# Attention with beacon keys and an ELU MLP on one core: sums of exp tiles and masks for both head pairs in one instruction, and a new written-out order

## The chip, the cores and the metric

The kernel runs on one core of a Trainium2 chip. Its engines work side by side: PE (TensorE, matmuls; PEld is its load of weights, which overlaps), DVE (VectorE), ACT (ScalarE), POOL (GpSimd) and SP (SyncE, which here only issues DMAs). The metric is the device time of one execution in microseconds, as the median of several runs.

## What is computed

Eight batches of attention with eight heads, 576 queries, 16 beacon keys ahead of 576 causal keys, and head size 64; then one MLP with an ELU on all 4608 tokens.

```python
# q, k, v: (8, 8, 576, 64); beacon_k, beacon_v: (8, 8, 16, 64)
k_all = concatenate([beacon_k, k], axis=2); v_all = concatenate([beacon_v, v], axis=2)
scores = where(causal, -1e9, q @ k_all^T / 8)      # beacons are never masked
a = exp(scores - max); a /= a.sum(-1) + 1e-9
x = (a @ v_all) as 4608 tokens x 512
h = x @ w_in                                       # 512 -> 2048
out = where(h > 0, h, exp(min(h, 0)) - 1) @ w_out  # 2048 -> 512, float32
```

## The kernel before

**Tiles.** The 592 keys of a batch stand in five chunks of up to 128 rows (the last has 80). Scores are computed with keys on the partitions, so that exp gives tiles that P·V takes as they are; only the causal part of each chunk is kept, 928 + 672 + 416 + 160 and, for the first chunk, 1152 columns for the two heads of a pair. The eight heads are four pairs, two pairs a group, and a group's exp tiles lie in one SBUF tile `et`. The MLP's 4608 tokens are tiles of 512 (the first cut in two halves, so the order counts tiles 0 to 9).

**Steps.** The order of the work is written out by hand: a list of words in `run(...)` (lines 790 on), each a small function with its arguments, and every engine runs its instructions in exactly that order. A word such as `S.3.6` is the function S for batch 3, piece 6. The words that matter here:

- `lq`, `T`, `cq`, `ck`: for batches 0 to 2, load q and k and transpose them on PE. From batch 3 on, `lk` (line 754) copies q (`.0`) or k (`.1`) of a batch into a scratch in HBM as bf16, issued by POOL, and `lt` (line 761) brings it back with DMA transposes issued by SP, two in a step, one step per group of heads, into the one pair of tiles `stq[1]`; `lp` (lines 769 and 770) fills the rest of the k tile: a memset and a copy of the beacon keys on POOL.
- `lv` (lines 144 and 149): the loads of V, five chunks and the beacons, issued by POOL into a tile `v16` that has two buffers. `wi` and `wo` (lines 161 and 165): the loads of the two weights, 16 and 4 pieces.
- `S` (line 320): scores on PE. `x` (335): exp on ACT. `m` (340): the causal mask, a multiplication on DVE.
- `D` (line 393), from batch 3 on: DVE adds a head pair's exp tiles over the chunks, so that `L` (lines 377 and 419) takes the row sums with one matmul a head from the result; `L` also does the first 112 queries of P·V. `n` (434, 437): reciprocals on ACT. `W` (377): the other queries of P·V. `M` (471): scaling on DVE into the MLP's input `xT`.
- `F` (511): the first MLP matmul, 4 x 128x512. `e`, `u` (521, 526) on ACT and `k`, `r`, `g` (536, 543, 548) on DVE: the ELU.
- `G` (557), tiles 0 and 1: the second MLP matmul. `Q` (621), the other tiles: the same in a form with seven instead of eight block products; `wt` and `Z` (578) are its additions on DVE, `J` (630, 635, 637) the drains of its sums, with stores issued by SP from a buffer `osb`. `H`, `X`, `P`, `K`, `E`, `U`, `V` do the first MLP matmul of the last two tiles in the same form.
- `o`, `s` (564, 570): drain and store of tiles 0 and 1.

POOL's transfers use eight completion semaphores in turn: each transfer is issued only when the one issued eight before it has landed.

The sums of `D` go to `presum[b, p]`, which is the buffer of a head pair that the transposes of batches 0 to 2 had used:

```python
r_ = presum[b, p] = qks[p % 2].bitcast(FP16)[:, :, 0:S]
...
o = r_[0:rows, :, a:e]
(nc.vector if eng == "v" else nc.gpsimd).tensor_tensor(
    out=o, in0=t[0:rows, :, a:e] if n == 0 else o, in1=t[0:rows, :, col:col + e - a], op=ALU.add)
```

Of the kernel before, what the change touches and what calls it, by code (L numbers as in the profile page):

```python
# [9 lines left out]
FP16 = mybir.dt.float16  # L10
# [7 lines left out]
def kernel(  # L18
# [134 lines left out]

# [3 lines left out]
    def load_wi(c):  # L157
        f_ = slice(DF // 2 * c, DF // 2 * (c + 1))
        for g in range(2):
            for i in range(4):  # L160
                nc.gpsimd.dma_start(
                    out=w_in16[32 * i:32 * (i + 1), 2 * g:2 * g + 2, f_], in_=wi_v[i, :, g, :, f_])
# [18 lines left out]
    qks = [konst.tile([P, 2, P * NKC], BF16, name=f"qk{i}") for i in range(2)]  # L181
# [67 lines left out]
    @step  # L249
    def wi(c):  # L250
        load_wi(c)
# [87 lines left out]
    def mask(o, i):  # L339
        nc.vector.tensor_tensor(out=o, in0=o, in1=i, op=ALU.mult)  # L340
# [5 lines left out]
    def m(b, p, g):  # L346

        t = et(b, p)
        if b > 0:
            m_ = lambda c: triu[:, c:c + 2, :].unsqueeze(1).broadcast_to([P, 2, 2, P])  # L350
            if g == 0:
                mask(t[:, :, 0:2 * C1].rearrange("p h (j c) -> p h j c", j=2)[:, :, :, 0:P], m_(0))
            else:
                n_ = C3 - C2
                mask(t[:, :, C2 - n_ + P:C3 + P].rearrange("p h (j c) -> p h j c", j=2)[:, :, :, n_ - P:n_], m_(1))
                mask(t[0:kc[4], :, C4:ECOLS], triu[0:kc[4], 1:3, 0:ECOLS - C4])
            return
# [27 lines left out]
    @step  # L385
    def D_(b, p, n, eng="v"):

        r_ = presum[b, p] = qks[p % 2].bitcast(FP16)[:, :, 0:S]
        t = et(b, p)
        a, e, col = next((a, e, col) for (j, a, e, col) in lays[b] if j == n + 1)  # L390
        rows = kc[n + 1]
        o = r_[0:rows, :, a:e]
        (nc.vector if eng == "v" else nc.gpsimd).tensor_tensor(  # L393
            out=o, in0=t[0:rows, :, a:e] if n == 0 else o, in1=t[0:rows, :, col:col + e - a], op=ALU.add)
# [6 lines left out]
    def L(b, g):  # L401
# [12 lines left out]
        else:  # L414
            t = hd[b, g] = psum.tile([P, 1024], FP32, tag="S", name="lt")
            r_ = lt[b, g] = t[:, 512 - QA:512 - QA + S]
            if b >= BD:
                for i in range(4):
                    nc.tensor.matmul(
                        out=r_[32 * i:32 * (i + 1), QA:S], lhsT=ones,  # L420
                        rhs=presum[b, 2 * g + i // 2][:, i % 2, QA:S], start=True, stop=True, skip_group_check=True)
# [374 lines left out]
    cb.1.3 r.0.4 g.0.4 e.1.7 r.1.7 lq.2.0.0.8 G.0.0.0 x.1.7 F.0.5 x.1.11 e.0.5 S.1.12 g.1.7
    cb.2.1 m.1.2.0 x.1.12 S.1.0 F.0.7 r.0.5 G.0.1.0 S.1.8 x.1.0 g.0.5 F.1.5 e.0.7 x.1.8 m.1.3.1
    S.1.10 cb.2.0 m.1.1.1 S.1.9 e.1.5 x.1.10 r.0.7 g.0.7 cb.2.2 lv.1.0.1 wo.1 r.1.5 g.1.5 x.1.9
    F.1.0 u.1.0 e.1.0 m.1.0.0 T.2.0.0 cq.2.0.0 F.0.3 T.2.1.0 cq.2.1.0 T.2.2.0 e.0.3 u.0.3
    m.1.2.1 k.0.3 wt.1.0 k.1.1 ck.2.2.0 F.1.4 F.0.6 e.0.6 S.2.0 S.2.5 x.2.5 x.2.0 r.0.6 m.1.3.0  # L800
    G.0.0.1 m.1.0.1 g.0.6 G.0.1.1 k.1.0 lv.1.2.3.4 lp.3.0 lp.3.1 T.2.3.0 e.1.4 ck.2.3.0 L.1.1
    n.1.1 F.1.2 r.1.4 u.1.2 e.1.2 M.1.1.0 W.1.1 M.1.1.1 S.2.3 F.1.3 x.2.3 L.1.0 W.1.0 n.1.0 wo.2
    M.1.0.0 M.1.0.1 u.1.3 e.1.3 wo.3 g.1.4 G.0.0.2 S.2.1 x.2.1 F.2.13 wt.1.1 e.2.13 S.2.4 lk.3.0
    lk.3.1 lt.3.0 x.2.4 S.2.8 x.2.8 k.1.2 cb.2.3 G.0.1.2 F.2.0 u.2.0 u.2.13 S.2.7 x.2.7 k.1.3
    S.2.9 x.2.9 e.2.0 G.0.0.3 o.0.0 G.0.1.3 F.2.3 e.2.3 S.2.10 m.2.0.0 S.2.2 r.2.3 g.2.3 k.2.0
    x.2.10 x.2.2 G.1.0.0 F.2.11 e.2.11 u.2.11 S.2.6 S.2.12 lv.2.2.3.4 x.2.6 F.2.1 u.2.1 e.2.1
    m.2.1.0 F.1.6 G.1.0.1 m.2.2.1 x.2.12 k.2.13 F.2.7 e.2.7 m.2.0.1 m.2.1.1 k.2.11 u.2.7 k.2.7
    u.1.6 lv.2.0.1 e.1.6 G.1.0.2 S.3.0 x.3.0 S.2.11 x.2.11 F.2.9 F.2.15 e.2.9 H.1.1 o.0.1 u.2.15
    k.2.1 k.1.6 m.2.3.0 e.2.15 L.2.0 W.2.0 n.2.0 F.2.12 m.2.3.1 r.2.9 g.2.9 M.2.0.1 lk.5.1 F.2.6
    M.2.0.0 G.1.0.3 lk.4.0 wt.2.0 wt.2.1 m.2.2.0 e.2.6 u.2.6 wt.4.1 s.0.0 s.0.1 u.2.12 e.2.12  # L810
    k.2.15 S.3.2 S.3.3 x.3.3 F.2.4 F.2.14 x.3.2 k.2.12 u.2.14 L.2.1 n.2.1 W.2.1 e.2.4 M.2.1.0
    M.2.1.1 e.2.14 u.2.4 G.1.1.0 S.3.4 F.2.2 lv.3.0.1 F.2.8 k.2.4 k.2.14 x.3.4 k.2.6 e.2.2 u.2.2
    e.2.8 r.2.8 m.3.0.1 S.3.1 o.1.0 k.2.2 lt.3.1 S.3.5 x.3.5 F.2.10 e.2.10 G.1.1.1 x.3.1 u.2.10
    G.1.1.2 m.3.0.0 lk.4.1 D.3.0.0 S.3.8 x.3.8 S.3.6 x.3.6 k.2.10 g.2.8 D.3.0.1 lt.4.0 Z.2.3.0
    F.3.12 m.3.1.0 D.3.1.0 m.3.1.1 e.3.12 G.1.1.3 H.1.2 D.3.1.1 u.3.12 S.3.9 o.1.1 s.1.1 S.3.11
    x.3.11 F.2.5 u.2.5 F.3.3 Q.2.0.7 e.2.5 k.2.5 x.3.9 k.3.12 Z.2.1.0 S.3.10 e.3.3 x.3.10 u.3.3
    k.3.3 F.3.1 Q.2.7.14 Z.2.2.0 m.3.2.1 Q.2.14.21 e.3.1 S.3.12 S.3.7 lt.4.1 u.3.1 x.3.12 F.3.13
    F.3.9 J.2.0.v x.3.7 e.3.13 Q.2.21.28 D.3.1.2 D.3.1.3 Z.2.3.1 Q.2.28.35 e.3.9 u.3.9 k.3.9
    D.3.0.2 D.3.0.3 k.3.1 wt.3.1 u.3.13 k.3.13 m.3.3.0 lp.4.0 S.4.4 x.4.4 S.4.0 F.3.0 x.4.0
# [113 lines left out]
```

## Time and profile before

| | |
|---|---|
| median of 3 runs | 337.73 us (336.92 to 338.57) |
| span of the profiled execution | 335.3 us, so about 2.4 us of the median lie around the span |
| PE | 324.6 us busy, 97%, 3561 matmuls |
| ACT | 282.5 us busy, 84% |
| DVE | 280.0 us busy, 84%, 592 instructions |
| POOL | 87.9 us busy, 26% |
| q0 (POOL's transfers) | 18.49 MB, mostly packets under 512 B |
| q1 (SP's) | 15.34 MB |

The profile is one execution, taken by the hardware profiler. Its page gives the busy time of each engine, the same in 40 equal slices (a digit is tenths of a slice, 9 for 90% or more; a slice here is 8.4 us), and groups of instructions by line and shape: `out<-in`, shape, count, then busy us and mean ns of one, then the idle time ahead of them and who ended it. A list of waits names for each engine and line whom it waited for, with the sum, the number and the longest. A list by windows gives, for a stretch of the span, the busy us of each engine, the mean clock of PE, the DMA share and the GB/s.

### The profile page before, as it was taken

The page shows a single profiled execution, that of the slowest core. Times are in us where ns is not written, and L with a number is a line of the kernel's source. Part 1 is how long each engine was busy: PE and PEld are TensorE (multiplying, and loading weights), DVE is VectorE, ACT ScalarE, POOL GpSimd, SP SyncE. Part 2 cuts the span into 40 slices and gives each one's busy share as a digit, 9 for nine tenths or more (in the row PEclk, how much of TensorE's full clock was granted, in tenths as well). Part 3 has the DMA queues.
Part 4 walks back from the last instruction along what each step waited for, and adds up shares of the span by engine and source line. Part 5 has one row for each costly group of instructions (what it writes and reads, how often), then busy time and mean ns, then how long its engine had stood idle before and what let it go on. Part 6 is the DMA issues. An engine that isn't in the chain of part 4 may idle for free.

```text
span 335.3 us, 8722 instructions
## 1 busy us (share of the span) xinstructions
PE 324.6 (97%) x3561; PEld 206.8 (62%) x3561; DVE 280.0 (84%) x592; ACT 282.5 (84%) x460; POOL 87.9 (26%) x121
## 2 busy tenths in 40 slices
PE   7979899999999999999999999999999999999995
PEld 3546666454446555657555656556555888688784
DVE  3652988666899999997999889988999998998962
ACT  2998798899999999989898889897987677988930
POOL 8875749360049106500160060000000000000000
PEclk9997999999999999999999999999999999999999
DMA  9999999999939997996099495000101021010212
GB/s 114 146 174 178 165 186 186 157 147 176 149 52 170 175 139 61 171 149 105 33 140 139 104 100 139 3 33 31 39 27 34 31 65 65 31 65 31 65 63 96
DMA packets 129080, 34.65 MB, mean 103 GB/s; under 512 B 112912, under 2 KB 127504, under 8 KB 129040
## 3 DMA queue, kind: packets, MB, share of 16 engines
q0 software_dynamic: 94912, 18.49, 68.6%
q1 hardware_dynamic: 33408, 15.34, 21.2%
q8 instruction: 28, 0.46, 0.6%
q10 hardware_dynamic: 720, 0.26, 0.3%
q14 instruction: 12, 0.10, 0.1%
HBM read 37.22 MB, written 15.34 MB: 157 GB/s over the span
## 4 chain that ended last, share of the span: by engine, by line
PE 53%; DVE 20%; ACT 11%; DMA 7%; POOL 4%; issue 3%; ACTq 0%; POOLq 0%
PE ops L621 20%; PE hps L511 16%; DVE gt L536 6%; PE hps L691 6%; DVE qk L393 5%; ACT et L335 4%; ACT e L521 3%; PE sc L320 3%; PE ops L557 3%; ACT r L526 3%; PE ut L377 3%; DMA v<-in_v_dram 2%; DMA kst<-in_k_dram 2%; DMA w_out<-in_moe_w_out_dram 2%; DVE et L340 2%
## 5 line engine op out<-in xcount | busy, mean ns | idle before, releaser
L511 PE MATMUL hps<-xT,w_in 128*128 128x512 f16 (+1 forms) x544 | 120.2, 357 | 0.7 <-DMA w_in<-in_moe_w_in_dram 0.5
L335 ACT ACTIVATE et<-sc 128x1024 f16<-128x1024 f32 (+2 forms) x114 | 104.7, 978 | 5.3 <-PE sc L320 5.3
L621 PEld LDWEIGHTS <-gt 128*128 128x128 f16 x768 | 74.1, 98 | 18.7 <-issue 1.7
L521 ACT ACTIVATE e<-hps 128x512 f32<-128x512 f32 x120 | 72.5, 622 | 7.7 <-PE hps L511 5.9
L511 PEld LDWEIGHTS <-w_in 128*128 128x128 f16 x544 | 49.8, 98 | 45.3 <-issue 7.9
L536 DVE SCALAR_TENSOR_TENSOR gt<-e,r 128x512 f16<-128x512 f32 x108 | 71.9, 682 | 6.7 <-ACT r L526 4.4
L526 ACT ACTIVATE r<-hps 128x512 f16<-128x512 f32 x108 | 65.3, 623 | 7.7 <-PE hps L511 4.4
L621 PE MATMUL ops<-wt,gt 128*128 128x256 f16 x384 | 50.1, 273 | 0.0
L621 PE MATMUL ops<-w_out,gt 128*128 128x256 f16 x384 | 49.6, 273 | 0.4 <-DVE osb L635 0.3
L149 POOL DMA_DIRECT2D v<-in_v_dram x40 | 36.0, 1048 | 5.5 <-DMA w_out<-in_moe_w_out_dram 2.4
L340 DVE TENSOR_TENSOR et<-et,triu 128x512 f16<-128x512 f16 (+4 forms) x108 | 31.6, 331 | 1.5 <-ACT et L335 1.5
L578 DVE TENSOR_TENSOR gt<-gt 128x1024 f16<-128x1024 f16 x48 | 32.4, 684 | 0.3
L393 DVE TENSOR_TENSOR qk<-qk,et 128x672 f16<-128x672 f16 (+2 forms) x60 | 21.8, 368 | 0.9
L377 PEld LDWEIGHTS <-v 128*32 128x32 f16 (+1 forms) x800 | 17.0, 96 | 8.7 <-issue 0.8
L377 PE MATMUL ut<-et,v 128*32 128x464 f16 (+3 forms) x560 | 21.0, 296 | 0.0
L637 DVE TENSOR_TENSOR osb<-ops,sm 128x512 f32<-128x512 f32 x24 | 16.4, 682 | 4.3 <-issue 3.3
L471 DVE TENSOR_TENSOR xT<-ut,rl 128x672 f16<-128x672 f32 (+12 forms) x26 | 16.4, 668 | 1.7 <-ACT rl L437 1.1
L621 PE MATMUL ops<-w_out,s 128*128 128x256 f16 x128 | 17.1, 273 | 0.0
L730 DVE SCALAR_TENSOR_TENSOR gt<-e,r 128x512 f16<-128x512 f32 x24 | 16.0, 685 | 0.8 <-ACT r L720 0.7
L144 POOL DMA_DIRECT2D v<-in_beacon_v_dram x8 | 6.5, 812 | 38.4 <-PE ut L377 38.4
L557 PE MATMUL ops<-w_out,gt 128*128 128x512 f16 x64 | 16.0, 380 | 0.6 <-DMA w_out<-in_moe_w_out_dram 0.6
L621 PEld LDWEIGHTS <-s 128*128 128x128 f16 x128 | 12.4, 98 | 3.0
(108 smaller groups left out, 394.8 us busy)
## 6 DMA issues: line engine op xcount, KB each, us to landing
out_dram<-osb SPq DMA_DIRECT2D x35, 256.0 KB, 2.3
v<-in_v_dram POOLq DMA_DIRECT2D x24, 128.0 KB, 7.1
scr<-in_q_dram POOLq DMA_DIRECT2D x5, 576.0 KB, 13.8
scr<-in_k_dram POOLq DMA_DIRECT2D x5, 576.0 KB, 15.4
w_in<-in_moe_w_in_dram POOLq DMA_DIRECT2D x16, 128.0 KB, 7.5
w_out<-in_moe_w_out_dram POOLq DMA_DIRECT2D x4, 512.0 KB, 9.4
v<-in_v_dram POOLq DMA_DIRECT2D x8, 112.0 KB, 9.7
v<-in_v_dram POOLq DMA_DIRECT2D x8, 80.0 KB, 6.7
```

Of the source, the lines that this page charges most:

```text
L149: nc.gpsimd.dma_start(out=vt[b][r0:r0 + n, j, :, :], in_=v[b, :, ilo[j]:ilo[j] + n, :].rearrange("h s d -> s h d"),)
L335: nc.scalar.activation(out=ets[b, d][:, :, a - EC2 * d:e - EC2 * d], in_=sc[b, g][:, :, a - c0:e - c0], func=AFT.Exp, bias=0.0, scale=SCALE)
L340: nc.vector.tensor_tensor(out=o, in0=o, in1=i, op=ALU.mult)
L377: nc.tensor.matmul(out=t[32 * i:32 * (i + 1), a - qa:e - qa], lhsT=ones[0:kc[j], :] if half is None else v16[0:kc[j], j, h, 32 * half:32 * ...
L393: (nc.vector if eng == "v" else nc.gpsimd).tensor_tensor(out=o, in0=t[0:rows, :, a:e] if n == 0 else o, in1=t[0:rows, :, col:col + e - a], ...
L511: nc.tensor.matmul(out=h[:, n_, :], lhsT=w_in16[:, cc, P * fc:P * (fc + 1)], rhs=xt[k][:, cc, a - TT * k:e - TT * k], start=(cc == 0), sto ...
L521: nc.scalar.activation(out=eb[t, i], in_=flat(hp[t, i]), func=AFT.Exp, bias=0.0, scale=1.0)
L526: nc.scalar.activation(out=rb[t, i], in_=flat(hp[t, i]), func=AFT.Relu, bias=0.0, scale=1.0)
L536: nc.vector.scalar_tensor_tensor(out=half(t, i), in0=eb[t, i], scalar=1.0, in1=rb[t, i], op0=ALU.subtract, op1=ALU.min)
L557: nc.tensor.matmul(out=ob[t, tb_], lhsT=gt[:, fc, P * tb_:P * (tb_ + 1)], rhs=w_out16[:, fc, :], start=(fc == 0), stop=(fc == NFC - 1))
L578: (nc.vector if eng == "v" else nc.gpsimd).tensor_tensor(out=o_, in0=a_, in1=b_, op=op_)
L621: nc.tensor.matmul(out=xy[t, n_][:, qd, :], lhsT=lw[:, P * qd:P * (qd + 1)], rhs=wt_[:, c, :], start=(first and qd == 0 and c == 0), stop= ...
```

## The change

1. `D` adds both head pairs of a group in one instruction: `D.b.p.n` becomes `D.b.g.n`, 80 instructions of 928, 672, 416 and 160 elements a partition become 40 of 1856, 1344, 832 and 320. The two buffers for the sums become one tile, and `L` reads its part of it. (A branch for batches under 3 is written but not used.)
2. `m`, for batches from 1 on, masks both pairs of a group at once: per batch 12 instructions become 6, those of 512 elements become 1024, those of 160 become 320.
3. The loads of V can be ordered chunk by chunk, with the beacons' load right behind chunk 0 rather than first; the loads of w_in are named one by one, in the same order as before.
4. The list of steps is new behind the first 160 or so. Matmuls, ACT's work and transfers are the same in number and bytes.

```diff
     def load_v(b, js):
         if b not in vt:
             vt[b] = stage.tile([P, NKC, H, D], FP16, tag="v16", name="v16")
-            nc.gpsimd.dma_start(
-                out=vt[b][0:NB, 0, :, :], in_=beacon_v[b].rearrange("h n d -> n h d"))
         for j in js:
...
+            if j == 0:
+                nc.gpsimd.dma_start(
+                    out=vt[b][0:NB, 0, :, :], in_=beacon_v[b].rearrange("h n d -> n h d"))
...
-    qks = [konst.tile([P, 2, P * NKC], BF16, name=f"qk{i}") for i in range(2)]
+    qk01 = konst.tile([P, 2, 2, P * NKC], BF16, name="qk01")
+    qks = [qk01[:, i, :, :] for i in range(2)]
...
-        t = et(b, p)
+        t = et(b, p) if b == 0 else None
         if b > 0:
-            m_ = lambda c: triu[:, c:c + 2, :].unsqueeze(1).broadcast_to([P, 2, 2, P])
+            t = ets[b, p].rearrange("p h (y c) -> p h y c", y=2)
+            m_ = lambda c: triu[:, c:c + 2, :].unsqueeze(1).unsqueeze(1).broadcast_to([P, 2, 2, 2, P])
             if g == 0:
-                mask(t[:, :, 0:2 * C1].rearrange("p h (j c) -> p h j c", j=2)[:, :, :, 0:P], m_(0))
+                mask(t[:, :, :, 0:2 * C1].rearrange("p h y (j c) -> p h y j c", j=2)[:, :, :, :, 0:P], m_(0))
...
-    def D_(b, p, n, eng="v"):
-
-        r_ = presum[b, p] = qks[p % 2].bitcast(FP16)[:, :, 0:S]
-        t = et(b, p)
+    def D_(b, g, n):
+
...
+            r_ = qk01.bitcast(FP16)[:, :, :, 0:S]
+        presum[b, g] = r_
+        t = ets[b, g].rearrange("p i (y c) -> p y i c", y=2)
...
-                        rhs=presum[b, 2 * g + i // 2][:, i % 2, QA:S], start=True, stop=True, skip_group_check=True)
+                        rhs=presum[b, g][:, i // 2, i % 2, QA:S], start=True, stop=True, skip_group_check=True)
```

The steps on POOL's queue between 33 us and the transfers of batch 5, in the order of issue:

```
before  wo.0 lq.2 lv.1.0.1 wo.1 lv.1.2.3.4 lp.3.0 lp.3.1 wo.2 wo.3 lk.3.0 lk.3.1 lv.2.2.3.4 lv.2.0.1
        lk.5.1 lk.4.0 lv.3.0.1 lk.4.1 lp.4.0 lv.3.2.3.4 lv.5 lp.4.1 lk.5.0 lk.6.0 lv.4 lk.6.1
after   wo.0 lq.2 wo.1 lv.1.1 lv.1.0 lv.1.4 lv.1.2 lp.3.0 lv.1.3 lk.3.1 lv.3.3 wo.2 lv.3.4 lk.3.0 wo.3
        lv.2.3 lv.2.2 lv.2.0 lp.3.1 lv.3.1 lv.2.4 lk.4.0 lv.2.1 lk.7.1 lk.7.0 lk.4.1 lk.6.1 lv.3.2
        lv.4.2 lv.3.0 lv.4.0 lv.4.3 lk.5.1 lp.4.0 lv.4.4 lk.5.0 lp.4.1 lk.6.0 lv.5.2 lv.4.1 lv.5.0
```

and on SP's:

```
before  lt.3.0 s.0.0 s.0.1 lt.3.1 lt.4.0 s.1.1 lt.4.1 J.2.1 lt.5.0 ... s.1.0 (beside tile 7)
after   lt.3.0 lt.3.1 s.0.0 lt.4.0 lt.4.1 s.0.1 J.2.1 s.1.0 lt.5.0 ...
```

The order of PE's steps around them, before:

```
G.0.0.2 S.2.1 F.2.13 S.2.4 S.2.8 G.0.1.2 F.2.0 S.2.7 S.2.9 G.0.0.3 G.0.1.3 F.2.3 S.2.10 S.2.2 G.1.0.0
F.2.11 S.2.6 S.2.12 F.2.1 F.1.6 G.1.0.1 F.2.7 G.1.0.2 S.3.0 S.2.11 F.2.9 F.2.15 L.2.0 W.2.0
```

and after:

```
G.0.1.1 G.0.1.2 S.2.6 S.2.1 F.2.0 F.2.11 S.2.4 S.2.10 G.0.0.1 G.0.0.2 F.1.6 F.2.13 S.2.2 S.2.9 F.2.3
G.0.1.3 L.2.0 F.2.15 F.2.9 S.2.11 S.2.12 G.0.0.3 F.2.1 S.2.8 S.2.7 G.1.0.0 F.2.7 G.1.0.1 F.2.6 S.3.3
S.3.0 F.2.14 F.2.12 W.2.0
```

More of the change, by code (lines that the diff above doesn't have):

```diff
@@ L152, in load_v, with load_wi @@
             )
+            if j == 0:
+                nc.gpsimd.dma_start(
+                    out=vt[b][0:NB, 0, :, :], in_=beacon_v[b].rearrange("h n d -> n h d"))
     wi_v = moe_w_in.rearrange("(g i t d) f -> i d g t f", i=4, t=2, d=32)
     wo_v = moe_w_out.rearrange("(f p) m -> p f m", p=P)
-    def load_wi(c):
+    def load_wi(c, n):
         f_ = slice(DF // 2 * c, DF // 2 * (c + 1))
[L159 to L162, printed above, removed]
+        g, i = n // 4, n % 4
+        nc.gpsimd.dma_start(
+            out=w_in16[32 * i:32 * (i + 1), 2 * g:2 * g + 2, f_], in_=wi_v[i, :, g, :, f_])
     def load_wo(i):
@@ L249, in wi @@
     @step
-    def wi(c):
-        load_wi(c)
+    def wi(c, n):
+        load_wi(c, n)
     @step
@@ L346, in m @@
     def m(b, p, g):
-        t = et(b, p)
+        t = et(b, p) if b == 0 else None
         if b > 0:
-            m_ = lambda c: triu[:, c:c + 2, :].unsqueeze(1).broadcast_to([P, 2, 2, P])
+            t = ets[b, p].rearrange("p h (y c) -> p h y c", y=2)
+            m_ = lambda c: triu[:, c:c + 2, :].unsqueeze(1).unsqueeze(1).broadcast_to([P, 2, 2, 2, P])
             if g == 0:
-                mask(t[:, :, 0:2 * C1].rearrange("p h (j c) -> p h j c", j=2)[:, :, :, 0:P], m_(0))
+                mask(t[:, :, :, 0:2 * C1].rearrange("p h y (j c) -> p h y j c", j=2)[:, :, :, :, 0:P], m_(0))
             else:
                 n_ = C3 - C2
-                mask(t[:, :, C2 - n_ + P:C3 + P].rearrange("p h (j c) -> p h j c", j=2)[:, :, :, n_ - P:n_], m_(1))
-                mask(t[0:kc[4], :, C4:ECOLS], triu[0:kc[4], 1:3, 0:ECOLS - C4])
+                mask(t[:, :, :, C2 - n_ + P:C3 + P].rearrange(
+                    "p h y (j c) -> p h y j c", j=2)[:, :, :, :, n_ - P:n_], m_(1))
+                mask(t[0:kc[4], :, :, C4:ECOLS],
+                     triu[0:kc[4], 1:2, 0:ECOLS - C4].unsqueeze(1).broadcast_to([kc[4], 2, 2, ECOLS - C4]))
             return
@@ L385, in D_ @@
     @step
-    def D_(b, p, n, eng="v"):
-        r_ = presum[b, p] = qks[p % 2].bitcast(FP16)[:, :, 0:S]
-        t = et(b, p)
+    def D_(b, g, n):
+        if b < BD:
+            r_ = stq[b % 2][g].bitcast(FP16)[:, 0:4 * S].rearrange("p (y i s) -> p y i s", y=2, i=2)
+        else:
+            r_ = qk01.bitcast(FP16)[:, :, :, 0:S]
+        presum[b, g] = r_
+        t = ets[b, g].rearrange("p i (y c) -> p y i c", y=2)
         a, e, col = next((a, e, col) for (j, a, e, col) in lays[b] if j == n + 1)
         rows = kc[n + 1]
-        o = r_[0:rows, :, a:e]
-        (nc.vector if eng == "v" else nc.gpsimd).tensor_tensor(
-            out=o, in0=t[0:rows, :, a:e] if n == 0 else o, in1=t[0:rows, :, col:col + e - a], op=ALU.add)
+        o = r_[0:rows, :, :, a:e]
+        nc.vector.tensor_tensor(
+            out=o, in0=t[0:rows, :, :, a:e] if n == 0 else o, in1=t[0:rows, :, :, col:col + e - a], op=ALU.add)
     op["D"] = D_
@@ new lines @@
+    G.1.1.2 e.2.5 F.3.9 u.2.5 F.3.7 x.3.5 lv.3.0 u.3.9 m.3.0.0 S.3.11 e.3.9 k.2.5 m.3.0.1 S.3.7
+    G.1.0.3 x.3.11 F.3.12 D.3.0.0 G.1.1.3 x.3.7 D.3.0.1 o.1.0 D.3.0.2 e.3.7 S.3.8 u.3.7 lv.4.0 k.3.7
+    lv.4.3 e.3.12 D.3.0.3 s.0.0 u.3.12 S.3.12 o.1.1 x.3.8 F.3.4 k.3.12 Q.2.0.7 Z.2.1.1 L.3.0 lk.5.1
+    e.3.4 m.3.1.0 lt.4.0 n.3.0 x.3.12 Q.2.7.14 wt.3.0 F.3.13 Q.2.14.21 u.3.13 lp.4.0 S.4.4 M.3.0.0
+    k.3.9 W.3.0 x.4.4 Z.2.1.0 Z.2.2.0 u.3.4 J.2.0.v lt.4.1 M.3.0.1 k.3.4 lv.4.4 D.3.1.0 S.4.1 x.4.1
@@ new lines @@
+    P.9.2.6 Q.8.91.98 V.9.2.4 U.9.2.5 U.9.2.6 F.9.14 E.9.2.6 Z.9.3.0 Z.9.1.0 Q.8.98.105 e.9.14
+    V.9.2.6 u.9.14 E.9.2.5 F.9.12 u.9.12 F.9.15 J.8.5 V.9.2.5 e.9.12 u.9.15 e.9.15 k.9.12
+    Q.8.105.112 k.9.14 F.9.13 k.9.15 Z.9.3.1 J.8.6 e.9.13 u.9.13 k.9.13 Q.9.0.7 Q.9.7.14 Q.9.14.21
+    Z.9.1.1 Q.9.21.28 Z.9.2.0 J.9.0 Q.9.28.35 Z.9.2.1 J.9.1 Q.9.35.42 Q.9.42.49 J.9.2 Q.9.49.56
+    Q.9.56.63 Z.9.4.1 Q.9.63.70 Z.9.4.0 Q.9.70.77 J.9.3 Q.9.77.84 Q.9.84.91 J.9.4 Q.9.91.98
+    Q.9.98.105 Q.9.105.112 Jh.9.0 J.9.5 Jh.9.1
```

224 lines of the change are left out of this document (103 added, 121 removed).

## The prediction

> **What bounds the kernel now.** I read the busy shares first, then the slices.
>
> ```profile
> PE 324.6 (97%) x3561; PEld 206.8 (62%) x3561; DVE 280.0 (84%) x592; ACT 282.5 (84%) x460; POOL 87.9 (26%) x121
> PE   7979899999999999999999999999999999999995
> DVE  3652988666899999997999889988999998998962
> PEclk9997999999999999999999999999999999999999
> DMA  9999999999939997996099495000101021010212
> ```
>
> PE is the bound: full from the fifth slice on, at full clock. No matmul is taken away, so a gain can only be PE's idle time. I priced each of PE's 474 steps by its median distance to the next step's start (0.86 us for a step F, 1.43 for W, 0.76 for seven matmuls of Q) and summed: 319.1 us in both orders, the switches between 128-row and 32-row or 64-row work included (75 before, 74 after). With 1.3 us ahead of the first matmul and 4.9 from the last one's start to the end, some 10 of the 335.3 us are waits, about 6 of them before 41 us, where order and loads stay nearly as they were. What is left is about 3.5 us, plus 0.6 at the first G. So the ceiling of any gain is near 4 us, 1.2%. Next, the waits from 40 us on:
>
> ```profile
> PEld L419 <- DVE qk L393: 1.5, 3, 0.6
> PE ops L557 <- DMA w_out<-in_moe_w_out_dram: 0.6, 1, 0.6
> PE lt L419 <- DVE qk L393: 0.4, 1, 0.4
> ```
>
> The columns are total, times and longest. Row sums (L419) wait for the sums that the change joins, 1.9 us, and G for the first chunk of w_out. Last the groups by shape (busy, mean ns):
>
> ```profile
> L393 DVE TENSOR_TENSOR qk<-et 128x928 f16<-128x928 f16 x20 | 12.7, 633 | 0.3 <-ACT et L335 0.2
> L393 DVE TENSOR_TENSOR qk<-qk,et 128x672 f16<-128x672 f16 x20 | 10.0, 501 | 0.2
> L393 DVE TENSOR_TENSOR qk<-qk,et 128x416 f16<-128x416 f16 x20 | 7.4, 370 | 0.3
> L393 DVE TENSOR_TENSOR qk<-qk,et 80x160 f16<-80x160 f16 x20 | 4.5, 234 | 0.3
> L340 DVE TENSOR_TENSOR et<-et,triu 128x512 f16<-128x512 f16 x56 | 22.9, 415 | 1.5 <-ACT et L335 1.5
> L340 DVE TENSOR_TENSOR et<-et,triu 80x160 f16<-80x160 f16 x32 | 7.4, 230 | 0.0
> L578 DVE TENSOR_TENSOR gt<-gt 128x1024 f16<-128x1024 f16 x48 | 32.4, 684 | 0.3
> ```
>
> and the stretch in which the transfers are the second bound (us, PE to POOL busy, clock, DMA share, GB/s), with SyncE's queue:
>
> ```profile
> 67.00:76.00 9.00, 9.00 (x72) 4.56 (x69) 6.02 (x14) 9.00 (x16) 6.29 (x5) 1.00 2.02 158
> 83.00:92.00 9.00, 9.00 (x115) 4.23 (x114) 7.06 (x14) 8.25 (x14) 0.00 (x0) 1.00 1.70 157
> 94.00:97.00 3.00, 3.00 (x22) 1.40 (x21) 2.75 (x8) 3.00 (x5) 0.50 (x2) 1.00 0.00 0
> ```
> ```profile
> 62.91 5.58 SPq L761 DMA_TRANSPOSE qst<-scr  x2
> 80.05 7.74 SPq L761 DMA_TRANSPOSE kst<-scr  x2
> ```
>
> From 33 to 93 us the queues move some 157 GB/s without a pause; by 94 they are empty, because POOL stands 20 us at step lp of batch 4.
>
> **Part 1, joined instructions.** Starts of back-to-back adds and masks lie 152 ns (160 elements), 334 (512), 552 (928) and 602 (1024) apart: 66 ns plus 0.523 ns an element. Two adds per chunk cost 2 x 1405 ns over the four shapes, one joined set 2540: 0.27 us saved per group, 2.7 over ten groups. 42 masks fewer at 66 ns: 2.8. Floor 5.5 us. By the durations (adds: 2 x 1738 against 1117+853+590+318, from 150 ns plus 0.52 an element) it is 6 each, 12. The stride over two pairs might cost the rate, but the 128x1024 step Z at 684 ns has strides of its own, and I take the floor. All this lies beside PE: DVE's own work, summed up to any add, stands 25 to 50 us below PE's work up to the L that reads it. DVE isn't short of time; PE waits at L419 because of where the last add of a group stands. So the 5.5 us are worth on the path only the waits they shorten: of the 1.9 us at L419 and the smaller ones on drains (0.33 ahead of a Q of tile 3), I take 1.2 regained. Bounds: nothing (the new order packs the last add as close to its L), 3.5 (all waits after 41 us gone). What is late next is PE itself.
>
> **Part 2, split loads of V and w_in.** Same transfers and bytes, 16 pieces of w_in in the same order. Only batch 0's beacon V is issued four transfers later, between chunks 0 and 1. Chunk 1, for which PE waited 0.3 us (landed 20.5, the first W at 20.6), has the same bytes ahead of it, so I take zero; as the beacons alone are 0.3 us of transfer, the bounds are ±0.3.
>
> **Part 3, the order from 36 us on.** PE, ACT and DVE get the same work (steps H, Z, J in the same number). G.0.0.0 now stands behind two half F and three S more, 2.5 us, more than the 0.6 that it waited for wo.0 (landed 40.2): 0.6 regained, bounds 0.4 to 0.7.
>
> POOL's queue is where it can lose. Before: batch 1's V, lp.3, wo.2, wo.3, both copies of batch 3, V of batch 2, lk.5.1, lk.4.0, two pieces of V 3, lk.4.1, the 20 us wait, the rest. After: batch 1's V, lp.3.0, lk.3.1, one piece of V 3, wo.2, another, lk.3.0, wo.3, then (behind a wait for W.1.0) V 2 in five pieces with lp.3.1, a piece of V 3 and lk.4.0 between, lk.7.1, lk.7.0, lk.4.1, lk.6.1, a piece of V 3, then lv.4.2, which waits for W.2.1, and only behind it the first chunk and beacons of V 3. So three copies for batches 6 and 7 (not needed before 150 us) stand ahead of V that step L of batch 3 reads. POOL allows eight transfers in flight.
>
> Prices, from landings in the trace: a scratch copy 3.7 us (62.8 to 66.5), a chunk of w_out 2.6 (56.4 to 59.0), a piece of V 0.9, 80 rows 0.6, beacons 0.3; and a pair of transposes takes 4.7 us from the others (13.0 us from 66.5 to 79.5 for 8.3 us of copies). Adding these in the new order from batch 1's V (53.9, as before), against PE's arrival by its own sum plus before's lag:
>
> - wo.2 61.1 for G.0.1.2 at 61.3, wo.3 68.2 for G.0.1.3 at 70.3: in time, the first just.
> - V 2, first chunk and beacons: 73.1 (72 to 75) for L.2.0 at 72.0, which before came only at 79.9: **1.1 us** waited.
> - lt.3.0: 78 for S.3.3 at 80.6; lt.3.1: 86.5 to 91 for S.3.9 at 93.1: in time.
> - last piece of V 2: 84 (82.5 to 87) for W.2.0 at 83.0 plus that 1.1: 0 to 3, **0.5** taken.
> - V 3's first chunk: 107 for L.3.0 at 105.5 plus 1.6: about 0.
> - lt.4.0 behind S.3.5: 109.5 for S.4.4 at 108.1 plus 1.6, lt.4.1 behind S.3.12: 116 for S.4.8 at 115.0 plus 1.6: **0.6** (0 to 2).
>
> On SP, s.0.1 now stands behind lt.4.1; J.2.1 needs its buffer, and would find the store landed near 117 against 115.5 plus 2.2: 0. s.1.0 moves from 280 to near 120, where SP has room. Behind a waiting PE every later step shifts alike, so what one wait costs is taken off the next (the 1.1 and 1.6 above), and the terms add: 2.2 (bounds 0, if all land at their early ends, and 7). Behind 117 us all landings have margin.
>
> One rule bears on the 13.0 us: the Trainium skill ("DMA: Bandwidth & Descriptors", section "Queues, rings and completion order") says that an engine takes turns between queue rows, a packet each. The trace differs: beside the transposes POOL's queue kept 38 to 86 GB/s against 80 to 124 on SyncE's, about 40%. With equal turns, V 2 would land near 83 and the sum would be about half a microsecond less.
>
> **Sum.** Span 335.3 − 1.2 − 0.6 + 2.2 = 335.7. The span is 2.4 us under the median of the runs shown, 337.7 (1.6 to 3.3 by lowest and highest); I add 2.4: **338.1**.
>
> **Rivals.**
>
> *Faster (R1).* All transfers arrive in time. For it: the estimates miss PE's arrival by 1 us, within their error, and 94 to 97 us was empty. Against it: five landings would all have to fall early. −0.6 and −1.2 to −3.5: spans 331.2 to 333.5, **333.6 to 335.9**, say 335.
>
> *Slower (R2): V of batch 3 lands late.* Its first chunk stands behind three copies for batches 6 and 7, 11.1 us, which the old order kept for later, and behind the pair lt.3.1 in the same stretch. I put it at 107 by summing; each pair took between 9 and 13 us to land under load, so 3 to 5 us more are in reach: 110 to 112. PE's order is fixed, and everything behind L.3.0 stands still too. It decides from a landing past 108.8 (105.5 plus the 1.6 of earlier waits, plus 1.7 that makes it visible). Against it: by the sum alone the queue has room, and 94 to 97 us was empty before. 338.1 + 3 to 5: **341 to 343**.
>
> *Slower (R3): ACT.* Between 84 and 133 us ACT was already without a pause; by sums of starts the new order leaves it 8.0 to 9.3 us of slack where it had 9.5 to 10.7. If its exp tiles end last, PE waits at a few steps S for sc's buffer (two in all), on top of the forecast by the 1.5 us that the slack shrank, up to twice that: 339.5 to 341. It decides where the slack is used up. Against it: behind 41 us no wait of PE over 0.1 us names ACT.
>
> *The joined form runs at half rate.* At 1.05 ns an element beyond the 66 a joined set of adds would cost 4.8 us instead of 2.5 and a large mask 1.1 instead of 0.6: 23 and 15 us more on DVE, 303 of 335 by starts. Each of the ten L of batches 3 to 7 would find its adds about 2 us later, up to 20 us on the path where nothing is shifted ahead: 340 to 355. Step Z's row speaks against it: 2 in 100.
>
> **How the numbers follow.** Same as before 0.34 (own range 336.0 to 339.4), R1 0.28, R2 0.24, R3 0.12, half rate 0.02. A difference under 0.5%, 1.7 us, can't be told from none here. The range leaves out the low end of R1 and R2's far end with the half rate: 334.4 to 342.6. Faster 0.28, same 0.34, slower 0.38.
>
> **What would show it.** Right: L393 x40 near 1.1, 0.85, 0.59 and 0.32 us, L340's large form near 0.68, DVE near 270 busy; no wait at L419 on L393; PE waiting at L377 or L419 for a DMA of V between 70 and 85 us, and at L320 for transposes near 109, 2 us in all. Wrong: PE without such waits (R1); one of them over 3 us (R2); waits on et or sc from ACT between 80 and 130 us (R3).

## The result, and the profile after

The changed kernel takes 338.69 us (median of 15 runs, 337.10 to 340.35) beside 337.11 us of the kernel before in the same rounds (335.88 to 339.38). The ratio is 1.0048, 95% interval 1.0029 to 1.0066: 1.6 us slower, 1.0 to 2.2. The profiled execution has a span of 337.9 us. One run below (joined instructions in the old order) was profiled in one of its two executions, out of twelve, that took 345 to 346 us; its ratio is of the other ten.

Busy time of the engines after the change:

```profile
PE 324.2 (96%) x3561; PEld 207.8 (61%) x3561; DVE 273.9 (81%) x510; ACT 282.5 (84%) x460; POOL 92.0 (27%) x121
```

The joined instructions do what the diff says. Their groups (count, busy us, mean ns of one):

```profile
L401 DVE TENSOR_TENSOR qk<-et 128x1856 f16<-128x1856 f16 x10 | 11.2, 1120 | 0.3 <-ACT et L336 0.3
L401 DVE TENSOR_TENSOR qk<-qk,et 128x1344 f16<-128x1344 f16 x10 | 8.5, 851 | 0.1
L401 DVE TENSOR_TENSOR qk<-qk,et 128x832 f16<-128x832 f16 x10 | 5.9, 588 | 0.2
L401 DVE TENSOR_TENSOR qk<-qk,et 80x320 f16<-80x320 f16 x10 | 3.2, 317 | 0.1
L341 DVE TENSOR_TENSOR et<-et,triu 128x1024 f16<-128x1024 f16 x28 | 19.2, 685 | 5.3 <-ACT et L336 5.1
```

DVE has 82 instructions fewer and is 6.1 us less busy. PE, the engine that bounds the kernel, has the same work and waits longer. Its longer waits from 30 us on (us in total, times, longest):

```profile
PE tp L267 <- DVE qk L280: 1.2, 1, 1.2
PE sc L321 <- DMA kst<-scr: 1.0, 1, 1.0
PE hps L519 <- DVE gt L556: 0.8, 2, 0.6
PE tp L267 <- DMA w_in<-in_moe_w_in_dram: 0.5, 1, 0.5
...
PEld L427 <- DVE qk L401: 0.3, 1, 0.3
```

The waits for the row sums' operand, 1.9 us before, are down to 0.3. The 0.6 us for w_out at the first G is gone. In their place stand three that the kernel before did not have: a transpose of batch 2 waits 1.2 us for a drain on DVE (L280), the scores of batch 4 wait 1.0 us for the DMA transposes, and a step F (F.0.5) at 39.9 us waits 0.6 for an ELU on DVE.

To see what these add up to I priced each PE step by the usual distance to the next start (35th percentile over both profiles, warm-up matmuls left out) and added what a step took beyond that, stage by stage. The end is the distance from the start of the last step Q to the end of the span.

| us beyond the price of the steps | before | after | after − before |
|---|---|---|---|
| up to 41 us | 9.7 | 9.4 | −0.3 |
| 41 to 60 us | 0.2 | 1.9 | +1.7 |
| 60 to 130 us | 0.6 | 1.9 | +1.3 |
| 130 us to the last Q | 3.3 | 1.9 | −1.4 |
| price of the steps in this order | | | +0.3 |
| from the last Q to the end | 4.94 | 5.86 | +0.9 |
| the whole span, for comparison | 335.3 | 337.9 | +2.6 |

The rows are rounded and add up to 2.5 of the 2.6. They add up by construction, since every distance is split into a price and a rest. With other ways of pricing (by the step that follows, or without it) the rows behind 60 us move by up to 0.5 us and the price of the order by up to 0.9; those of 41 to 60 us and of the end stay. The medians of the time differ by only 1.6: the profiled execution of the changed kernel took 339.73 us, 1.0 above its median, and the largest piece of its 41 to 60 us stage does not come in every execution, as is shown below.

### The profile page after: what moved, and what is told of

It is laid out like the page before. It is cut to its first block, busy times and chain, and to the rows that moved or that the text cites. A ratio compares the mean times of both kernels' runs of the same rounds, so it can differ in the third digit from the quotient of the medians.

```text
span 337.9 us, 8639 instructions
## 1 busy us (share of the span) xinstructions
PE 324.2 (96%) x3561; PEld 207.8 (61%) x3561; DVE 273.9 (81%) x510; ACT 282.5 (84%) x460; POOL 92.0 (27%) x121
## 3 DMA queue, kind: packets, MB, share of 16 engines
q0 software_dynamic: 94912, 18.49, 65.9%
q1 hardware_dynamic: 33408, 15.34, 20.4%
HBM read 37.22 MB, written 15.34 MB: 156 GB/s over the span
## 4 chain that ended last, share of the span: by engine, by line
PE 69%; ACT 9%; DVE 9%; DMA 6%; POOL 3%; issue 2%; SPq 0%; DVEq 0%; POOLq 0%
PE hps L519 25%; PE ops L629 24%; PE sc L321 6%; ACT et L336 5%; PE hps L699 4%; PE ut L381 4%; DMA kst<-scr 3%; PE ops L565 3%; DMA v<-in_v_dram 3%; ACT e L529 2%; DVE gt L556 1%; ACT r L534 1%; PE lt L381 1%; POOL kst L136 1%; POOL qst L136 1%
## 5 line engine op out<-in xcount | busy, mean ns | idle before, releaser
L336 ACT ACTIVATE et<-sc 128x1024 f16<-128x1024 f32 (+2 forms) x114 | 106.0, 982 | 6.0 <-PE sc L321 5.8
L529 ACT ACTIVATE e<-hps 128x512 f32<-128x512 f32 x120 | 73.8, 631 | 7.3 <-PE hps L519 6.6
L519 PEld LDWEIGHTS <-w_in 128*128 128x128 f16 x544 | 50.5, 98 | 42.9 <-issue 6.6
L534 ACT ACTIVATE r<-hps 128x512 f16<-128x512 f32 x108 | 66.3, 627 | 7.9 <-PE hps L519 6.4
L147 POOL DMA_DIRECT2D v<-in_v_dram x40 | 35.0, 884 | 44.4 <-PE ut L381 30.3
L341 DVE TENSOR_TENSOR et<-et,triu 128x1024 f16<-128x1024 f16 (+5 forms) x66 | 27.1, 449 | 5.3 <-ACT et L336 5.1
L401 DVE TENSOR_TENSOR qk<-qk,et 128x1344 f16<-128x1344 f16 (+2 forms) x30 | 17.6, 585 | 0.3
L762 POOL DMA_DIRECT2D scr<-in_k_dram x5 | 11.5, 2305 | 14.5 <-issue 10.0
```

Of the source, the lines that this page charges most:

```text
L147: nc.gpsimd.dma_start(out=vt[b][r0:r0 + n, j, :, :], in_=v[b, :, ilo[j]:ilo[j] + n, :].rearrange("h s d -> s h d"),)
L336: nc.scalar.activation(out=ets[b, d][:, :, a - EC2 * d:e - EC2 * d], in_=sc[b, g][:, :, a - c0:e - c0], func=AFT.Exp, bias=0.0, scale=SCALE)
L519: nc.tensor.matmul(out=h[:, n_, :], lhsT=w_in16[:, cc, P * fc:P * (fc + 1)], rhs=xt[k][:, cc, a - TT * k:e - TT * k], start=(cc == 0), sto ...
L529: nc.scalar.activation(out=eb[t, i], in_=flat(hp[t, i]), func=AFT.Exp, bias=0.0, scale=1.0)
L534: nc.scalar.activation(out=rb[t, i], in_=flat(hp[t, i]), func=AFT.Relu, bias=0.0, scale=1.0)
```

## The experiments

Each was timed in five rounds beside the kernel before; ratios are to that. Each edited kernel ran twelve times, except the second one with joined instructions in the old order, which ran nine times.

**The two halves of the change.** First the joined instructions in the old order, each put where the later of its two predecessors stood:

```diff
-m.3.0.0 lk.4.1 D.3.0.0 S.3.8 x.3.8 S.3.6 x.3.6 k.2.10 g.2.8 D.3.0.1 lt.4.0 Z.2.3.0 F.3.12 m.3.1.0 D.3.1.0 m.3.1.1
+lk.4.1 S.3.8 x.3.8 S.3.6 x.3.6 k.2.10 g.2.8 lt.4.0 Z.2.3.0 F.3.12 m.3.0.0 D.3.0.0 m.3.0.1
```

> Parts 1 alone: the joined D and m in the old order, each at the place of the later of the two that it replaces; loads and everything else as before. Theory (the joined instructions gain a little, the new order loses it): DVE about 6 us less busy, PE's waits at the row sums (1.9 us before) down to 0.3 to 1.9, so 0 to 1.5 us less than before, ratio 0.995 to 1.000. Rival (the joined instruction itself costs, because the last add of a group takes 0.32 instead of 0.23 us and masks stand later): 0.5 to 1.5 us more than before, with longer waits at the row sums, ratio 1.002 to 1.005.

Measured: 1.0043 (1.0016 to 1.0071). This is the rival's side. Then the new order, with two instructions again in each step D and m (the cut shows D; m is split alike):

```diff
-        o = r_[0:rows, :, :, a:e]
-        nc.vector.tensor_tensor(
-            out=o, in0=t[0:rows, :, :, a:e] if n == 0 else o, in1=t[0:rows, :, :, col:col + e - a], op=ALU.add)
+        for y in range(2):
+            o = r_[0:rows, y, :, a:e]
+            nc.vector.tensor_tensor(
+                out=o, in0=t[0:rows, y, :, a:e] if n == 0 else o, in1=t[0:rows, y, :, col:col + e - a], op=ALU.add)
```

> The new order with the sums and masks made pair by pair again (two instructions where the changed kernel has one). Theory (the order brings the loss and the joined form only shortens waits): the changed kernel's waits of 1.3 us at the transposes of batch 2, 1.0 at the first scores of batch 4's second half and the later end all stay, and DVE's 6 us come back, 0 to 2 us more than the changed kernel, ratio to before 1.005 to 1.011. Rival (the joined form is what loses): at or under the kernel before, ratio 0.998 to 1.001.

Measured: 1.0040 (1.0017 to 1.0064), a little under the expected 1.005 and not to be told from the whole change. By its time, the new order alone is as slow as both together. Of the three places that were expected to stay, its profiled execution (337.83 us, 0.85 under the median) has only the late end: T.2.3.0 waits 0.2 us and S.4.8 not at all. Behind 130 us PE's waits sum to 2.2 us here and to 1.9 in the changed kernel, against 3.3 before: the order shortens them by 1.1, and the joined form by 0.3 more. One thing is in no trace: in all 12 executions 2.0 to 2.15 us of the time lie outside the span, against 1.7 to 1.9 in the changed kernel and the kernel before. So 0.3 us of this kernel's time are not in its waits, and why is not shown.

The joined form in the old order was run once more with step r in another form (that edit is below, for another reason):

> Joined D and m in the old order, with step r in that form. In the profile without it, r.1.5 took 4.46 us while POOL issued both copies of batch 3, PE waited 3.7 us, and behind 130 us PE waited 4.6 us against 3.3 before. Theory A (the loss of 1.4 us of the joined instructions in the old order is that collision): it goes, ratio 0.997 to 1.000. Theory B (the joined instructions stand where the later of two stood and hold DVE up for longer, so that drains and sums come late): the waits behind 130 us stay 1 to 1.5 us above before's, ratio 1.003 to 1.005.

Measured: 1.0075 (1.0045 to 1.0105), theory B. Its waits behind 130 us show where (this is the view of PE's and PEld's waits in that stretch):

```profile
PE lt L427 <- DVE qk L401: 0.7, 2, 0.5
...
PEld L427 <- DVE qk L401: 2.5, 5, 0.7
```

Row sums now wait 3.2 us, seven times, for the last joined add, against 1.9 us in four before. A joined set starts only when the later pair's masks are through, and its last add takes 0.32 us rather than 0.23; in an order made for single adds it ends late. Fewer and longer instructions saved DVE 6.1 us (275.4 busy, against 281.5 in the kernel before with the same form of r) and cost PE 0.9 us of waits behind 130 us against that kernel (4.6, 3.7), or 1.3 against the kernel before (3.3).

**The end.** J.9.5, the add and the store of the next to last 256 KB, stands behind Jh.9.0 in the new order. In the changed kernel SP's queue ends like this (start, us issuing):

```profile
330.29 0.37 SPq L648 DMA_DIRECT2D out_dram<-osb  x1
333.40 0.34 SPq L751 DMA_DIRECT2D out_dram<-osb  x1
333.84 0.39 SPq L648 DMA_DIRECT2D out_dram<-osb  x1
```

J.9.5's sums are ready by 332 (DVE adds them at 331.26, for 0.69 us), but its store is issued at 333.84, behind the 128 KB of Jh.9.0, which waits for the very last matmul. Before, the big store was already out:

```profile
328.63 2.06 SPq L640 DMA_DIRECT2D out_dram<-osb  x2
331.74 0.34 SPq L743 DMA_DIRECT2D out_dram<-osb  x1
```

```diff
-Q.9.98.105 Q.9.105.112 Jh.9.0 J.9.5 Jh.9.1
+J.9.5 Q.9.98.105 Q.9.105.112 Jh.9.0 Jh.9.1
```

> The changed kernel with one step moved: J.9.5 (DVE's add and SP's 256 KB store) ahead of the last two Q, as it was before, instead of behind Jh.9.0. Theory: its store no longer stands in SP's queue behind the store that waits for the very last drain, and the end comes 1.0 us after the last matmul sooner (4.9 instead of 5.9 us): 0.8 to 1.2 us less than the changed kernel, ratio to before 1.001 to 1.002. Rival (the end is set by the last drains anyway): no change from the changed kernel, 1.005.

Measured: 1.0005 (0.9984 to 1.0027), and 4.96 us from the last Q's start to the end instead of 5.86. The same step moved the other way in the kernel before:

```diff
-J.9.5 Q.9.98.105 Q.9.105.112 Jh.9.0 Jh.9.1
+Q.9.98.105 Q.9.105.112 Jh.9.0 J.9.5 Jh.9.1
```

> The kernel before with J.9.5 behind Jh.9.0, as the changed kernel has it. Theory (the store of 256 KB behind the last drain's store is worth 1.0 us by itself): 0.8 to 1.2 us more than before, ratio 1.002 to 1.004, the end 5.9 instead of 4.9 us behind the start of the last Q. Rival (the 1.4 us of the run of the tail were noise): within 0.3 us of before.

Measured: 1.0053 (1.0026 to 1.0079) and 5.88 us. By the ratios the two runs moved 1.4 and 1.8 us, more than the 0.9 us of the traces, but with intervals that hold it. One store in the wrong place on SP is 0.9 us, the largest lasting piece of the loss. With the store back in its place the changed kernel can't be told from the kernel before.

**The transpose that waits for DVE.** The drain (L280) that T.2.3.0 waits for stands behind r.0.7, which took 1.87 us in the changed kernel's profile (the others of its kind 0.42 to 0.43). DVE's and POOL's instructions at that time:

```profile
46.97 1.87 DVE L551 TENSOR_SCALAR r<-e 128x512 f16<-128x512 f32 x1
48.95 0.69 DVE L556 TENSOR_TENSOR gt<-hps,r 128x512 f16<-128x512 f32 x1
```
```profile
46.40 2.19 POOL L762 DMA_DIRECT2D scr<-in_k_dram  x1 [2.04 <-DMA kst<-in_k_dram]
```

r ended 0.25 us after POOL had done issuing the copy of k (lk.3.1, to 48.59). The profile of the joined form in the old order has it larger, with several of POOL's issues back to back:

```profile
46.85 4.46 DVE L551 TENSOR_SCALAR r<-e 128x512 f16<-128x512 f32 x1
```
```profile
46.27 2.24 POOL L762 DMA_DIRECT2D scr<-in_q_dram  x1
47.98 2.76 POOL L762 DMA_DIRECT2D scr<-in_k_dram  x1
49.67 1.73 POOL L144 DMA_DIRECT2D v<-in_beacon_v_dram  x1
50.19 3.71 POOL L149 DMA_DIRECT2D v<-in_v_dram  x3
```

This r ended at 51.31, 0.6 us behind the second copy's issue, while those of V went on. PE then waited 3.7 us for the ELU, and the granted clock was 0.50 from 52 to 58 us: the next half F took 1.86 us instead of 1.03. Priced as in the table, this profile loses some 6 us between 41 and 60 us. So I put lk.3.1 one place back:

```diff
-lk.3.1 G.0.1.0 g.0.5 x.1.9 lv.3.3
+G.0.1.0 g.0.5 x.1.9 lv.3.3 lk.3.1
```

> The changed kernel with lk.3.1 (POOL's 2.2 us of issuing the copy of k of batch 3) one place later, behind lv.3.3 (0.9 us). In the changed kernel the step r.0.7 on DVE took 1.87 us instead of 0.43 while POOL issued lk.3.1. Theory (POOL's issue holds DVE up): r.0.7 0.4 to 0.9 us, the wait ahead of T.2.3.0 from 1.2 to under 0.4, 0.8 to 1.3 us less than the changed kernel, ratio to before 1.001 to 1.002. Rival (r.0.7 is long for what it reads, or the transposes wait because their drains stand late on DVE): r.0.7 still 1.5 to 1.9 us, no change, 1.005.

Measured: 1.0027 (1.0009 to 1.0045). r.0.7 took 0.46 us and T.2.3.0 did not wait. But the interval overlaps that of the changed kernel, and the profiles of the split kernel and of the moved store, which leave lk.3.1 where it is, don't have the wait either: in the one POOL began to issue at 43.69, too early to meet r, in the other r.0.7 ran from 47.41 to 47.83 inside an issue that had begun at 47.28, and was not held. The profile of the run below that puts three later copies back has the collision again, and the 1.2 us at T.2.3.0 with it:

```profile
46.04 1.85 DVE L551 TENSOR_SCALAR r<-e 128x512 f16<-128x512 f32 x1
```
```profile
45.45 2.19 POOL L762 DMA_DIRECT2D scr<-in_k_dram  x1 [2.00 <-DMA kst<-in_k_dram]
```

So it is in two of the four profiles that leave lk.3.1 and r as the change has them. It is a matter of tenths of a microsecond, and what moving lk.3.1 is worth in the median is not shown. Next, r in a form that reads a second tensor, as step k does:

```diff
-        nc.vector.tensor_scalar(
-            out=rb[t, i], in0=eb[t, i], scalar1=1.0, scalar2=1.0, op0=ALU.min, op1=ALU.subtract)
+        nc.vector.scalar_tensor_tensor(
+            out=rb[t, i], in0=eb[t, i], scalar=1.0, in1=ones[:, 0:1].broadcast_to([P, 512]),
+            op0=ALU.min, op1=ALU.subtract)
```

> The changed kernel with step r in another form: scalar_tensor_tensor with a column of ones as second tensor (as step k has it, which no run shows held up) instead of tensor_scalar. Theory (what POOL does while it issues a copy holds up only the tensor_scalar form): all 12 r take about 0.68 us and none more, no wait at T.2.3.0 in any execution, 0.3 to 1.0 us less than the changed kernel, ratio to before 1.001 to 1.004, and a narrower spread of the runs. Rival (r's time isn't what delays the transposes; 0.26 us more on each of 12 r costs in the stretch up to 60 us): 0 to 1 us more than the changed kernel, 1.005 to 1.008.

> The kernel before with step r in that form. Theory: its three r that took 0.71 to 1.04 us in the profile take 0.68 like the others; the executions over 340 us (two of 35) don't come; median within 0.6 us under before, ratio 0.998 to 1.000. Rival: 12 x 0.26 us more on DVE in a stretch in which PE waits for the first tiles: 0.3 to 1 us more, 1.001 to 1.003.

Measured: 1.0062 (1.0040 to 1.0085) in the changed kernel, 1.0006 (0.9986 to 1.0026) in the kernel before. All r take 0.68 or 0.69 us in this form and none took longer in the three profiles that have it. One of them, in the joined form in the old order, lies wholly inside the issue of a copy (71.41 to 72.10 in 70.93 to 73.13). As a cure the form is worth nothing: each r takes 0.26 us longer, the times of the changed kernel are no closer together (338.06 to 341.89), and T.2.3.0 still waits 0.4 us there without any collision. With the short form and no collision it waited 0.2 us at most (split kernel, moved store, lk.3.1 moved), so the longer r is the likelier reason; that was not tried by itself.

**The scores of batch 4.** S.4.8 waited 1.0 us for the second transposes of batch 4, which landed at 117.8. Three copies for batches 6 and 7 were put back in POOL's queue:

```diff
-lk.7.1 ... lk.7.0 ... lk.6.1 ... lk.6.0 ... lv.5.4
+lk.6.0 lk.6.1 ... lv.5.4 lk.7.1 lk.7.0
```

> The changed kernel with three of POOL's copies moved back in its queue: lk.6.1 behind lk.6.0, lk.7.1 and lk.7.0 behind lv.5.4, so that they no longer stand ahead of V of batch 3 and the transposes of batch 4. Theory (the wait of 1.0 to 1.1 us ahead of S.4.8 comes from those 11 us of copies): the second pair of transposes of batch 4 lands before PE arrives, that wait is gone, 0.8 to 1.2 us less than the changed kernel, ratio to before 1.001 to 1.002. Rival (the transposes are late because lt.4.1 is issued only behind S.3.12, whatever the copies do): the wait at S.4.8 stays over 0.7 us, 1.004 to 1.005.

Measured: 1.0030 (1.0007 to 1.0053). V of batch 3 landed 5 us earlier (97.7 instead of 102.6), the transposes of lt.4.1 hardly sooner behind their issue (12.3 us instead of 12.5), and the wait was still 0.7 us:

```profile
PE sc L321 <- DMA kst<-scr: 0.7, 1, 0.7
```

So the three copies are not the cause, as the rival had it. SP may issue lt.4.1 only behind S.3.12 (104.8 on PE in the changed kernel), the loaded pair landed 11.5 to 13 us behind its issue in all profiles of the new order, and PE is at S.4.8 12 us behind S.3.12. But the rival is not the whole cause either: in the kernel before the pair was issued at 104.9 as well and PE was at S.4.8 as long behind S.3.12, yet in the five profiles of the old order the pair landed 9.8 to 11.1 us behind its issue. What holds it up in the new order was not found. A candidate is the copies for batch 5, which POOL issues at 100.0 and 103.8 (lk.5.1 and lk.5.0) and which in the old order went out at 63.2 and 105.6.

**Together.** Four moves on the changed kernel, with S.4.8 some 2 us later on PE (behind S.4.2, a Q and an F) and s.0.1 in front on SP's queue:

```diff
-S.4.8 wt.4.0 S.4.2 J.2.1 D.3.1.1 x.4.2 s.1.0 u.3.1 x.4.8 Q.2.35.42 F.3.11
+wt.4.0 S.4.2 J.2.1 D.3.1.1 x.4.2 s.1.0 u.3.1 Q.2.35.42 F.3.11 S.4.8 x.4.8
-s.0.0 ... lt.4.1 ... s.0.1
+s.0.0 s.0.1 ... lt.4.1
-lk.3.1 ... lv.3.3
+lv.3.3 lk.3.1
-Q.9.98.105 Q.9.105.112 Jh.9.0 J.9.5
+J.9.5 Q.9.98.105 Q.9.105.112 Jh.9.0
```

> The changed kernel with four moves of steps: J.9.5 ahead of the last two Q (as in the run of the tail), lk.3.1 behind lv.3.3 (as in the run of the later copy), S.4.8 with its exp behind F.3.11 (1.8 us later on PE), and s.0.1 right behind s.0.0 on SP, so that J.2.1 finds its buffer once S.4.8 no longer holds PE. Theory (what the change lost is those places, and the rest of the new order gains the 1.2 us of waits behind 130 us): 1.0 + 1.0 + 0 to 0.7 less than the changed kernel, 336.0 to 336.7 beside 337.3 of before, ratio 0.995 to 0.998. Rival (PE meets the next late thing a step later): ratio 0.999 to 1.002, with a new wait between 115 and 125 us.

Measured: 0.9997 (0.9970 to 1.0025). It is as fast as the kernel before, not faster. The moved store alone had given 1.0005, so it is not shown that the three other moves are worth anything. The wait at S.4.8 is gone, and a new one stands in L.3.0, for the beacons of V of batch 3 (landed 106.3, L begun at 105.3):

```profile
PE lt L381 <- DMA v<-in_beacon_v_dram: 0.7, 1, 0.7
```

The same moves with the instructions split again:

> The same with sums and masks pair by pair again. Theory (in the new order the joined instructions only shorten a few waits behind DVE): 0 to 0.7 us more than with the joined ones, behind 130 us 2.2 us of waits instead of 1.9. Rival (DVE's 6 us matter once the other waits are gone): 1 to 3 us more, ratio 1.000 to 1.005.

Measured: 1.0031 (1.0004 to 1.0059). By the ratios the joined form is worth 1.1 us here, but the intervals overlap, the split form's waits behind 130 us are only 2.3 us against 2.0, and 0.3 us more of its time lie outside the span, as in the split kernel above; that the joined form is worth more than these two is not shown. At last the four moves with the three copies put back, as above:

> The four moves and the fifth, the three copies of batches 6 and 7 back in POOL's queue (lk.6.1 behind lk.6.0, lk.7.1 and lk.7.0 behind lv.5.4). With the four moves alone PE waited 0.7 to 1.0 us at step L of batch 3 for the first chunk and the beacons of V of batch 3 (landed 106.3, L begun at 105.3), which stand behind those copies. Theory (the copies put V there, and with it in time nothing else is late): that wait is gone, V of batch 3 lands before 100, 0.7 to 1.0 us less than the four moves, 336.1 to 336.5 beside 337.3 of before, ratio 0.996 to 0.999. Rival (the copies then collide with the transposes of batch 5 or 6, or PE meets the next late thing): a new wait of 0.5 us or more behind 110 us and a ratio of 0.999 to 1.002.

Measured: 1.0009 (0.9982 to 1.0036). V of batch 3 landed at 98.8 and behind 41 us no DMA is among PE's waits any more:

```profile
PE hps L519 <- DVE gt L556: 0.8, 2, 0.6
PE lt L427 <- DVE qk L401: 0.2, 1, 0.2
PE hps L519 <- ACT r L534: 0.2, 1, 0.2
```

Between 60 and 130 us PE waits 0.9 us instead of 1.8, and yet the time is not less. The table's method agrees that there was little to win against the kernel before: leaving out the wait of F.0.5, which stands for the one at the first G, this kernel waits 3.6 us behind 41 us against 4.1, and the price of its steps in this order is 0.45 us more, together about the same. No version here beats the kernel before by what five rounds can tell.

## Why the prediction was right, and where its steps were not

The forecast was no change, 338.1 us within 334.4 to 342.6; measured were 338.69 us and a ratio just under the half per cent. The interval (1.0029 to 1.0066) doesn't hold 1, though: 15 executions could tell apart what the forecast held too small to tell. That the sum came out so near is in part luck. Most of the 2.2 us of transfer waits did not come, and losses that the sum did not have, at the end and between 41 and 60 us, stood in their place.

- **The joined instructions' cost: right.** 1.12, 0.85, 0.59 and 0.32 us and 0.685 us are the forecast durations; DVE is 6.1 us less busy, between the floor of 5.5 and the 12 by durations. The half-rate rival is out.
- **1.2 us regained at waits for DVE: right in size, wrong in cause.** Behind 130 us 1.4 us were regained. But the new order with split instructions regains 1.1 of it, which leaves 0.3 to the joined ones, and in the old order these lose 0.9 to 1.3. The step that failed is "the 5.5 us are worth on the path only the waits they shorten". They could also lengthen waits, since a joined add can't begin before the later pair is ready and ends later. I had named its lower bound as nothing; in the old order it was below nothing.
- **0.6 us regained at the first G: not there.** That wait is gone, but F.0.5, now ahead of G, waits 0.6 us for an ELU on DVE at 39.9 us. The step looked at one transfer and not at what the step put in its place reads.
- **2.2 us of transfers: 1.0.** V of batch 2 landed at 71.1 for L.2.0 at 72.8 and at 83.1 for W.2.0 at 84.6, where 73.1 against 72.0 and 84 against 84.1 had been forecast: 1.6 us of waits that didn't come in this profile. The margin is small: in those of the moved store and of the four moves, joined and split, W.2.0 takes 0.2 to 0.6 us longer, with the last piece of V landed at 83.3 to 84.5. The price of a copy beside transposes was taken from a stretch at about 158 GB/s; from 41 to 70 us the queues move 172, and moved 175 in the kernel before. What came is the wait for lt.4.1, 1.0 us where 0.6 was given to both pairs of batch 4. V of batch 3, forecast at 107 and just in time, landed at 102.6, but in the run of four moves it was late, at 106.3: the place was the right one to watch, the three copies ahead of it the right cause. The prediction's test of equal turns between the queues compared GB/s, which can't decide on turns by the packet: in the kernel before POOL's queue moved 18.49 MB in 94912 packets and SyncE's 15.34 MB in 33408, so that a packet of the one carries less than half of the other's.
- **The 4.9 us behind the last Q: wrong, by 0.9 us.** I counted the end as unchanged and did not follow J.9.5 past Jh.9.0 on SP's queue. It can be read from the two orders alone.
- **41 to 60 us, left out: 1.7 us in the profiled execution, about 0.5 in the profiles without the collision.** I said that order and loads before 41 us stay and that the first losses come with V of batch 2. The transposes of batch 2 and the drains they wait for on DVE were moved too (forecast: nothing), and lk.3.1 was moved onto a step r.
- **The 2.4 us added to the span: mis-sized.** They do not lie around the span. In all executions of both kernels the time is 1.7 to 1.9 us above the span; the rest is that the profiled execution of the kernel before was quicker than its median. The sum would have been some 0.6 us lower, and still within the range.
- The rivals: R1 needs all transfers in time; all but lt.4.1 were, and still nothing was gained. R2's and R3's waits did not appear, ACT is named in no wait of PE over 0.2 us.

The Trainium skill has the rule that I passed over ("SBUF — State Buffer", section "SBUF: two separate sides"): VectorE in some forms and GpSimd share a port pair, whoever starts first has it for the whole instruction, and GpSimd needs it to write the descriptors of the transfers it issues. The runs agree in the main: of the two forms of r only the tensor_scalar was held, beside a single issue of a copy until 0.25 us after POOL was through (48.84 after 48.59, 47.89 after 47.64), and the two-tensor form never. They differ in one point: an r that began 0.13 us after POOL's issue wasn't held by the 2.2 us that followed, so the issue as the profile shows it isn't the hold from its start. Spans on POOL are rough in these profiles, so the tenths are not to be leaned on.

## What to carry to other kernels

Where PE was full, cutting instructions on another engine was worth little by itself: ask when the last of them ends, because a joined instruction starts with its later input, and give it an order of its own. When an order is new, follow every queue to its very end, SP's last stores too: one 256 KB store behind the last drain's store cost 0.9 us, and 6 us less of VectorE's work gave 0.3 in waits. And when DMAs issued by GpSimd are moved, look at which VectorE instructions run at that time.

## What was not expected of the hardware

- A tensor_scalar of 128x512 on VectorE (0.43 us) took 1.87 us beside one issue of a scratch copy by GpSimd (2.2 us) and 4.46 us beside several back to back; scalar_tensor_tensor on the same data took 0.68 or 0.69 in all 36 instructions of three profiles.
- GpSimd's small copies in step lp got longer in the new order: 0.75 and 1.04 us in the mean for the two tiles instead of 0.53 and 0.44, and 2.21 and 1.41 in the new order with split instructions. So it is not the joining. They were off the path; the cause was not tried.
- After 3.7 us without a matmul the granted clock was 0.50 for 6 us (joined form in the old order):

```profile
52.00:58.00 6.00, 5.83 (x66) 4.35 (x66) 4.80 (x8) 2.20 (x3) 3.61 (x5) 0.50 1.94 177
```

- The pair of DMA transposes lt.4.1 landed 12.5 us after its issue, and 11 us of copies taken out from ahead of it made that 12.3; in the kernel before it was 10.2.
